# Six whole-array tiles instead of four in the prologue of a dense squared-ReLU kernel, taken row tile by row tile, with w1's first chunks on ScalarE's queue

## Chip, cores, metric

One core of a Trainium2 chip. Kernels are compared only within the same rounds. The metric is the device time of one execution in microseconds (us). An execution's time is about 1.75 us longer than the span that the profile shows (290.45 against 288.7 for the profiled run of the kernel before).

## The reference

```python
B, S, D, F = 1, 2048, 576, 4608          # all bf16
def reference(x, w1, b1, w2, b2):
    h = jnp.einsum("bsd,df->bsf", x, w1) + b1
    r = jnp.where(h > 0, h, 0)
    h = r * r
    return jnp.einsum("bsf,fd->bsd", h, w2) + b2
```

## The kernel before

F is cut into 36 tiles of 128 columns ("f-tiles"), S into four blocks of 512 rows. The first phase makes h for all f-tiles of each block, the second multiplies by w2. D = 576 is 4.5 times 128, so the usual form of the first product is row-split: two f-tiles run side by side on the two 64-row halves of the array, nine chunks of 64 each (`a_step`, which comes down to line L213 in the profile). That form needs x transposed and in two halves. For block 0 x has to be transposed on the spot, so its first G = 4 f-tiles take a whole-array form: four chunks of 128 rows and one paired 64-row rest. They need less data and let the row-split weights arrive meanwhile.

```python
    load_x(nc.sync, 0)
    load_x(nc.scalar, 1)
    load_quad(nc.sync, 0)          # w1 rows of chunk c, columns of the first G f-tiles
    load_quad(nc.scalar, 1)
    load_quad(nc.sync, 2)
    load_x(nc.scalar, 2)
    load_x(nc.sync, 3)
    load_quad(nc.scalar, 3)
    nc.scalar.activation(out=warm[:], in_=..., func=ACT.Relu)     # brings the table load forward
    # ... (cut: the 64-row rest, then the row-split w1 chunks on SyncE, pair by pair)
    for i in range(NWARM):         # NWARM = 5: matmuls of ones while x is on its way
        nc.tensor.matmul(wps[:], lhsT=ones[:, 0:P], rhs=ones[:], start=(i == 0), stop=(i == NWARM - 1))

    def transpose_chunks(half, cs, engs):      # half = two row tiles of x
        tps = [psum.tile([P, HALF], BF16, name="tp", tag="bank") for c in cs]
        for i in range(2):
            for c, tp in zip(cs, tps):
                d0 = c * P if c < NC else D - P
                nc.tensor.transpose(tp[:, i * P:(i + 1) * P], xs[:, 2 * half + i, d0:d0 + P], ident[:])
        # ... (cut: copies from PSUM into xT[0])
    def full_mm(half, c):                      # 256 columns, G f-tiles
        for q in range(4):
            nc.tensor.matmul(bk0[q][:, cols], lhsT=qn[:, c, q * P:(q + 1) * P], rhs=xT[0][:, c, cols], ...)

    transpose_chunks(0, (0,), (V,))
    transpose_chunks(0, (1,), (A,))
    transpose_chunks(0, (2,), (A,))
    transpose_chunks(0, (NC,), (V,))
    full_mm(0, 0)
    transpose_chunks(0, (3,), (A,))
    full_mm(0, 1)
    # ... (cut: the rest in the same manner, b1's transpose, the paired 64-row rest, evictions)
    for j in range(2, NJ):
        a_step(0, j)
```

All PSUM tiles (PSUM is the memory that TensorE writes to) come from one pool of eight banks; a bank is free again when VectorE or ScalarE has copied its contents out.

## Time and profile before

| | |
|---|---|
| median of the first three runs | 290.14 us (289.88 to 290.80) |
| span of the profiled run | 288.7 us |
| TensorE busy | 284.9 us (99%) |
| first transpose, first row-split matmul | 2.71 us, 9.62 us |
| array goes from half to full clock | 5.95 us (the trace's clock record) |

In the timeline a line is: start, length, engine, source line, operation, operands, count, and in brackets idle time with what ended it. For TensorE the length includes draining, so two starts are subtracted to get a pitch: two 512-column matmuls of ones start 0.43 us apart at half clock, and row-split pairs 0.216 us apart at full clock. "tp" are transposes, "ph" accumulating matmuls, "wps" the warm-up; PE is TensorE, DVE VectorE, ACT ScalarE, and SP SyncE. The row "PEclk" of the page does not show the half clock of the start; its record begins at the switch. The pitch of the matmuls shows it.

### The profile page before, as it was taken

Reading aid. Unit: us, or ns where it says so; the run is one execution under the profiler, and the core shown is the slowest. Engines: PE = TensorE matmul, PEld = TensorE weight load, DVE = VectorE, ACT = ScalarE, POOL = GpSimd, SP = SyncE. Lnnn points to the kernel's source line nnn. Section 1 sums busy time; section 2 is a strip of 40 time slices with the busy share of each in tenths; the row PEclk is TensorE's granted clock in tenths of the full one; section 3 lists DMA queues with packets and bytes.
Section 4 is the critical chain, followed back from the end, with each engine's and each line's share of the span. In section 5 each row is a group of like instructions: output and inputs, shape, how many; then the busy total and the mean of one; then the engine's idle time right before and its main releaser. Section 6 shows DMA issues by size and latency. Waiting matters only on the chain.

```text
span 288.7 us, 4818 instructions
## 1 busy us (share of the span) xinstructions
PE 284.9 (99%) x2067; PEld 133.7 (46%) x2078; DVE 79.5 (28%) x196; ACT 95.6 (33%) x153; POOL 1.5 (1%) x8
## 2 busy tenths in 40 slices
PE   9999999999999999999999999999999999999996
PEld 5544444444444444444445444444444444444454
DVE  1644454444445444444420011111100111111111
ACT  3666666766666676666620000000000000000000
POOL 2000000000000000000000000000000000000000
PEclk9999999999999999999999999999999999999999
DMA  7999999910400004300000100000000000000000
GB/s 200 205 190 204 172 185 208 321 50 2 122 3 0 3 2 142 106 0 2 0 2 19 20 20 20 20 23 5 15 20 23 20 20 20 23 20 22 20 23 20
DMA packets 35381, 18.01 MB, mean 62 GB/s; under 512 B 21652, under 2 KB 35360, under 8 KB 35360
## 3 DMA queue, kind: packets, MB, share of 16 engines
q1 hardware_dynamic: 34752, 17.14, 26.4%
q10 hardware_dynamic: 576, 0.56, 0.6%
q8 instruction: 16, 0.26, 0.4%
q14 instruction: 5, 0.04, 0.0%
q0 software_dynamic: 32, 0.01, 0.0%
HBM read 11.94 MB, written 2.36 MB: 50 GB/s over the span
## 4 chain that ended last, share of the span: by engine, by line
PE 98%; DMA 1%; issue 0%; DVE 0%; ACTq 0%
PE ph L213 47%; PE po L329 43%; PE pc L315 5%; PE ph L228 2%; DMA w_sb<-in_x_dram 1%; PE tp L182 1%; PE ph L254 0%; DVE o_sb L331 0%; PE b1T_ps L247 0%; ACTq L353 0%
## 5 line engine op out<-in xcount | busy, mean ns | idle before, releaser
L197 ACT ACTIVATE r<-ph,b1T 128x512 bf16<-128x512 f32 x144 | 91.0, 685 | 48.4 <-PE ph L213 46.4
L213 PE MATMUL ph<-w_sb,w1h 64*128 64x512 bf16 x936 | 101.2, 376 | 0.0
L213 PEld LDWEIGHTS <-w1h 64*128 64x128 bf16 x1260 | 61.3, 94 | 74.6
L329 PE MATMUL po<-w_sb,hT 128*128 128x512 bf16 x423 | 92.9, 379 | 0.5
L329 PEld LDWEIGHTS <-hT 128*128 128x128 bf16 x432 | 42.2, 98 | 51.2 <-issue 0.4
L199 DVE TENSOR_TENSOR hT<-r 128x512 bf16<-128x512 bf16 x108 | 46.0, 426 | 54.7 <-ACT r L197 54.2
L331 DVE TENSOR_TENSOR o_sb<-po,b_bc 128x512 bf16<-128x512 f32 (+2 forms) x17 | 11.2, 660 | 116.7 <-PE po L329 109.7
L213 PE MATMUL ph<-xT,w1h 64*128 64x512 bf16 x324 | 35.1, 376 | 0.0
L329 PE MATMUL po<-w_sb,w1h 128*128 128x512 bf16 (+2 forms) x178 | 31.2, 336 | 0.1
L329 PEld LDWEIGHTS <-w1h 128*128 128x128 bf16 x180 | 16.2, 98 | 15.3
L199 DVE TENSOR_TENSOR w1h<-r 128x512 bf16<-128x512 bf16 x36 | 15.3, 426 | 19.6 <-ACT r L197 19.5
L315 PE MATMUL pc<-hT,w_sb 128*64 128x512 bf16 x108 | 15.7, 379 | 0.0
L315 PEld LDWEIGHTS <-w_sb 128*64 128x64 bf16 x144 | 8.1, 110 | 7.6 <-issue 0.4
L315 PE MATMUL pc<-w1h,w_sb 128*64 128x512 bf16 x36 | 7.9, 379 | 0.0
L317 ACT ACTIVATE oc<-pc,b2T 128x512 bf16<-128x512 f32 x2 | 1.4, 687 | 13.7 <-PE pc L315 13.7
L325 DVE COPY o_sb<-oc 128x64 bf16<-128x64 bf16 x16 | 2.8, 172 | 9.3 <-DMA oc<-oc 9.3
L228 PE MATMUL ph<-w_sb 128*128 128x256 bf16 x32 | 5.3, 313 | 0.0
L228 PEld LDWEIGHTS <-w_sb 128*128 128x128 bf16 x32 | 3.4, 115 | 0.6
L175 DVE COPY w_sb<-tp 128x256 bf16<-128x256 bf16 x5 | 1.5, 292 | 5.9 <-PE tp L182 5.9
L182 PE MATMUL tp<-ident,w_sb 128*128 128x128 bf16 x20 | 2.7, 264 | 0.1
L169 PE MATMUL wps<-one 128*128 128x512 bf16 x5 | 2.3, 628 | 0.4 <-DVE one L144 0.4
L182 PEld LDWEIGHTS <-w_sb 128*128 128x128 bf16 x20 | 1.9, 118 | 1.4 <-DMA w_sb<-in_x_dram 1.2
(27 smaller groups left out, 10.7 us busy)
## 6 DMA issues: line engine op xcount, KB each, us to landing
w_sb<-in_w_dram SPq DMA_DIRECT2D x2, 1728.0 KB, 8.7
w1h<-in_w_dram SPq DMA_DIRECT2D x8, 288.0 KB, 5.9
out_dram<-o_sb SPq DMA_DIRECT2D x15, 144.0 KB, 1.8
w1h<-in_w_dram SPq DMA_DIRECT2D x12, 144.0 KB, 3.7
w_sb<-in_w_dram SPq DMA_DIRECT2D x2, 864.0 KB, 7.2
w1h<-in_w_dram SPq DMA_DIRECT2D x2, 576.0 KB, 11.2
w_sb<-in_x_dram SPq DMA_DIRECT2D x2, 144.0 KB, 3.4
w_sb<-in_x_dram ACTq DMA_DIRECT2D x2, 144.0 KB, 3.5
```

What stands on the lines that cost most here:

```text
L169: nc.tensor.matmul(wps[:], lhsT=ones[:, 0:P], rhs=ones[:], start=(i == 0), stop=(i == NWARM - 1))
L175: nc.vector.tensor_copy(out=dst, in_=src)
L182: nc.tensor.transpose(tp[:, i * P:(i + 1) * P], xs[:, 2 * half + i, d0:d0 + P], ident[:])
L197: nc.scalar.activation(out=r[:], in_=bk[:], func=ACT.Relu, bias=b1T[:, ft:ft + 1], scale=1.0)
L199: nc.vector.tensor_tensor(out=hT_of(b, ft), in0=r3, in1=r3, op=ALU.mult)
L213: nc.tensor.matmul(bk[h][:], lhsT=w1h[rows, c, j * P:(j + 1) * P], rhs=xT[b][rows, place(h, c), :], start=(i == 0), stop=(i == NH - 1))
L228: nc.tensor.matmul(bk0[q][:, cols], lhsT=qn[:, c, q * P:(q + 1) * P], rhs=xT[0][:, c, cols], start=(half == 0 and c == 0), stop=False, ski ...
L315: nc.tensor.matmul(pc[h * H:(h + 1) * H, :], lhsT=w2(ft, DM, D), rhs=hT_of(2 * pr + h, ft), start=(ft == 0), stop=(ft == NFT - 1))
L317: nc.scalar.activation(out=oc[:, pr, :], in_=pc[:], func=ACT.Identity, bias=b2T[:], scale=1.0)
L325: nc.vector.tensor_copy(out=o_sb[:, DM:D], in_=o_tr[pr][:, jj, h * H:(h + 1) * H])
L329: nc.tensor.matmul(po[:, 0:e - a], lhsT=hT_of(b, ft)[:, jj, :], rhs=w2(ft, a, e), start=(ft == 0), stop=(ft == NFT - 1))
L331: nc.vector.tensor_tensor(out=o_sb[:, a:e], in0=po[:, 0:e - a], in1=b2_bc[:, a:e], op=ALU.add)
```

## The change

Its intent: run six f-tiles in the whole-array form, so that the row-split weights are wanted later; begin as soon as row tile 0 of x is there; put other matmuls between a tile's transposes and their first use; and ask for w1's chunks from ScalarE while SyncE asks for x.

```diff
-    G = 4
+    G = 6
+    GP = G // 2
-    load_x(nc.sync, 0)
-    load_x(nc.scalar, 1)
-    load_quad(nc.sync, 0)
-    load_quad(nc.scalar, 1)
-    load_quad(nc.sync, 2)
-    load_x(nc.scalar, 2)
-    load_x(nc.sync, 3)
-    load_quad(nc.scalar, 3)
+    for j in range(RT):
+        load_x(nc.sync, j)
+        load_quad(nc.scalar, j)
 ... (pairs and the row-split chunk list follow: single chunks for j = 3 to 9)
+    def transpose_tile(j, c, n, eng):          # row tile j, n chunks into one bank
+        ...
+    transpose_tile(0, 0, 1, V)
+    transpose_tile(0, 3, 1, V)
+    transpose_tile(0, 1, 2, A)
+    transpose_tile(0, NC, 1, V)
     bk0 = [bank("ph") for _ in range(G)]
+    full_mm(0, 1, 0)                           # row tile, number of row tiles, chunk
+    transpose_tile(1, 0, 2, V)
+    transpose_tile(1, 2, 2, A)
+    full_mm(0, 1, 1)
+    full_mm(1, 1, 0)
+    full_mm(1, 1, 1)
+    transpose_tile(2, 0, 2, V)
+    transpose_tile(2, 2, 2, A)
+    full_mm(0, 2, 2)
+    full_mm(2, 1, 0)
+    transpose_tile(1, NC, 1, V)
+    full_mm(2, 1, 1)
+    transpose_tile(3, 0, 2, V)
+    transpose_tile(3, 2, 2, A)
+    full_mm(2, 1, 2)
+    full_mm(0, 2, 3)
 ... (cut: the rest of row tile 3, b1, the paired 64-row rest)
-    for j in range(2, NJ):
+    for j in range(GP, NJ):
         a_step(0, j)
```

## The prediction

> **What bounds the kernel now.** I read the page first: busy time, the slices, then the chain that ended last.
>
> ```profile
> span 288.7 us, 4818 instructions
> PE 284.9 (99%) x2067; PEld 133.7 (46%) x2078; DVE 79.5 (28%) x196; ACT 95.6 (33%) x153; POOL 1.5 (1%) x8
> PE   9999999999999999999999999999999999999996
> PE 98%; DMA 1%; issue 0%; DVE 0%; ACTq 0%
> ...
> L213 PE MATMUL ph<-w_sb,w1h 64*128 64x512 bf16 x936 | 101.2, 376 | 0.0
> ```
>
> The reader is to see that TensorE is never free after the start: the chain is 98% TensorE, and the row-split matmuls of the first phase (L213) wait 0.0 us in all. Nothing that the change touches lies after the first of 18 steps of block 0, so only the first microseconds can move. For those I asked for the chain in time order, 0 to 30 us, and for TensorE's timeline of the same stretch.
>
> ```profile
> 0.21 2.84 DMA w_sb<-in_x_dram
> 3.04 0.05 issue
> 3.09 0.93 PE tp L182 x7
> 4.02 0.85 PE ph L228 x4
> 4.87 0.21 PE tp L182 x2
> 5.09 1.36 PE ph L228 x8
> 6.45 0.22 PE tp L182 x4
> 6.67 0.44 PE ph L228 x4
> ...
> 9.24 0.54 PE ph L254 x4
> 9.78 20.29 PE ph L213 x187
> ```
>
> The first rows are the arrival of x; from 3.09 us on every row is TensorE. The four 256-column matmuls at 4.02 us take 0.85 us (0.21 each), the four at 6.67 us take 0.44 (0.11 each). So the array runs at half speed until about 6 us; the trace's clock record puts the switch at 5.95 us. Evictions and weight arrivals do not show as waits:
>
> ```profile
> 2.71 1.31 PE L182 MATMUL tp<-ident,w_sb 128*128 128x128 bf16 x8
> 3.81 1.06 PE L228 MATMUL ph<-w_sb 128*128 128x256 bf16 x4
> 4.67 0.42 PE L182 MATMUL tp<-ident,w_sb 128*128 128x128 bf16 x2
> 4.88 1.57 PE L228 MATMUL ph<-w_sb 128*128 128x256 bf16 x8
> ...
> 9.17 0.60 PE L254 MATMUL ph<-w_sb 64*128 64x512 bf16 x4
> ```
>
> From start to start, there are three holes on TensorE: the last warm-up matmul starts at 2.06 and streams 0.43 us, so 2.49 to 2.71 is empty (0.22 us, row tile 0 of x lands); 2.82 to 3.09 (0.27 us; the second transpose wants row tile 1, which lands at 3.04); and about 0.09 us before 9.17. That is all an ideal reordering could win: 0.58 us of 290, or 0.2%. Two of the holes lie at half clock, where a hole costs half its length in full-speed work (if the switch stays at 5.95).
>
> **What the Trainium skill says.** "TensorE: Matmul & The Clock Gate", Part 1 (The HAM clock gate): the array is at half clock until a window of about 3.4 us has been busy; the window runs freely and "doesn't reset when your kernel starts", so the switch moves from run to run. The trace agrees on the two speeds (0.21 and 0.11 us) and has the switch at 5.95 us; that it moves, one trace cannot show, but the three times spread over 0.9 us. "DMA: Bandwidth & Descriptors", Issuing engines are not separate DMA queues: transfers started by ScalarE and SyncE run on the same 16 DMA engines and interleave. The trace agrees: both queues' packets alternate from 1.8 us on, and together move 331 GB/s from 1.8 to 4.2 us. The same page, Why small descriptors are slow, says that short descriptors pay a fixed overhead: here the first loads, with 1,024 and 1,152 B pieces, make those 331 GB/s, the later w1 chunks with 256 B pieces 196 GB/s (9.6 to 21.6 us).
>
> **The change part by part.**
>
> Work on TensorE. Before, one whole-array f-tile costs 8 matmuls of 256 columns (0.1085 us start to start) and half of a paired 512-column matmul (0.216/2), 0.98 us; a row-split pair of f-tiles costs 9 x 0.216 = 1.94 us, 0.97 each. So moving two f-tiles from one form to the other is free by itself. After, block 0's six tiles need 60 matmuls of 128 columns (transposes of that width run at 0.0545 us start to start, each with its own weights, so 60 x 0.0545 = 3.27), 18 of 256 columns (1.95) and three pairs (0.65): 5.87 us. Before, the same six tiles cost 4 x 0.976 + 1.94 = 5.85. Sum: +0.02 us. The 20 transposes and the one of b1 stay.
>
> Start. Only row tile 0 of x is needed for the first five transposes, so the 0.27 us hole for row tile 1 goes. In its place the first matmuls wait for the first eviction and w1's first chunk. Five transposes at half clock: 2.71 to 3.24. The first copy starts when the first transpose has drained (2.71 + 0.29 + 0.03 = 3.03). A VectorE copy of 256 columns from PSUM takes 292 ns (L175), the 36-column cast 195; between them 128 columns make an estimate of 0.24 us, so chunk 0 is ready at 3.27 and seen by TensorE around 3.33. w1's first chunk is now first on ScalarE's queue, where row tile 1 landed at 3.04 before; it has 197 KB for 147, an estimate of 3.2. The hole is 3.24 to about 3.4, 0.16 us instead of 0.27. Gain, at half clock: 0.06 us.
>
> Middle. The six accumulating banks leave two of eight for transposes, and the built program makes each new transpose wait for the eviction two before it. I walked the order with 0.107 us (cold) and 0.0545/0.1085 us (warm) per matmul. Tile 1's transposes at about 4.04 meet ScalarE's first copy, which cannot start before its warm-up ends at 3.63 and takes 0.37: ready at 4.05, a hole of at most 0.05. Tile 3's second pair of transposes meets a real one: the remainder transpose of tile 1 starts at about 7.4, drains by 7.6, and its two copies on VectorE (2 x 0.24) free the bank at 8.1, while TensorE has only 6 matmuls and 2 transposes in between (0.33 + 0.11) and stands there at 7.88. Hole: 0.2 us at full clock. The others (b1's transpose, tile 2's remainder) come out within 0.1 us of even.
>
> DMA. The first loads grow from 1,114 KB to 1,376 KB (w1 chunks of 768 columns instead of 512). At 331 GB/s that is +0.8 us, so w1's last chunk lands at about 6.6 instead of 5.9; it is first used at about 8.6, while before it was used 0.55 us after it landed. The order in which chunks are used leaves every one about a microsecond. The row-split chunks then start at pair 3, wanted at about 11.7 instead of 9.4; the bytes before the last, four-pair chunk are the same in sum, but 295 KB of them now move at 331 instead of 196 GB/s: about 0.6 us earlier. This is worth something only where a chunk is nearly late: before, the last half chunk landed at 32.69 and was read at 32.93, without a stall in this trace.
>
> Sum: +0.02 (work) - 0.06 (start) + 0.03 (tile 1) + 0.2 (tile 3) = +0.2 us, at most +0.3. The first row-split matmul should start at about 11.7, against 11.56 at which the same six f-tiles are done before. 290.14 + 0.2 would be 290.3; I take 290.2, as the DMA slack may save a stall in runs that the trace does not show.
>
> **The rivals.**
>
> First, the change hides real latency and gains its whole 0.6 us: for it speaks that x and w1 are now asked for in the order of use and that other work lies before each first use; against it, that the before trace shows no wait for an eviction on TensorE after 3.1 us. It would give 289.6.
>
> Second, the clock switch comes a window later, as narrower matmuls and holes between 2.5 and 6 us leave TensorE less busy when it is judged. For it speaks only that this stretch has more eviction waits; against it that its holes sum to 0.4 us by my walk, no more than before (0.5). A later switch by 3.4 us would cost 1.7 us: 291.9. I give it 5%.
>
> Third, DMA: heavier early loads delay row tiles 1 to 3 or push the row-split stream behind, and TensorE waits; per microsecond of delay not covered one microsecond is lost. For it speaks that SyncE's ninth load waits on the semaphore of ScalarE's first, now larger load (it waited 1.1 us before); against it the extra 2 us before the first row-split chunk is wanted. It would give 290.5 to 291.5.
>
> Fourth, a late w1 chunk already costs time in unprofiled runs before, and the 0.6 us earlier stream saves it: 289.4 to 289.8. The trace can neither show nor exclude it.
>
> **Range and chances.** A change of 2% is 5.8 us; block 0's whole prologue, up to the first row-split matmul, is 9.6 us of which 3.9 is useful work at full speed. The first rival's gain is a tenth of the 2% line and the worst rival's loss a third of it. So within 2% has 0.99, and 0.005 remains for each side. The range is set by the run-to-run spread (289.88 to 290.8 for the kernel before), widened to the low side by the first and fourth rival and to the high side by the third: 289.4 to 291.0 us around 290.2.
>
> **What would show it right or wrong.** In the changed trace: TensorE's first transposes at about 2.7; the first 128-column matmul at about 3.4, not later than 3.6; the clock switch near 6 us (a switch near 9.4 is the second rival); a wait of the second transposes of tile 3 on VectorE of about 0.2 us; L208 starting within 0.3 us of 11.7, and no idle time on it. If L208 starts before 11.3, my walk of the bank waits is too dark; if after 12.1, a DMA or a bank wait was missed. A gain over 1 us with these starts as predicted would mean that the row-split stream stalls in runs without a profile. The prediction as a whole is wrong if the median leaves the range.

## The result, and the profile after

The changed kernel took 290.31 us (median of 4 runs, 289.99 to 290.72) against 290.11 (4 runs, 289.88 to 290.80). Ratios here are the mean time of one kernel's fast runs over the mean of the other's in the same rounds, not quite the ratio of medians: 1.0004, 95% interval 0.9982 to 1.0025. Run again with five rounds it was 290.44 against 290.32, ratio 1.0002 (0.9988 to 1.0016).

The page of the changed kernel:

```profile
span 288.2 us, 4882 instructions
PE 284.2 (99%) x2097; PEld 134.3 (47%) x2108; DVE 80.4 (28%) x202; ACT 94.8 (33%) x152; POOL 1.5 (1%) x8
PE 97%; ACT 1%; issue 0%; DVE 0%
...
L208 PE MATMUL ph<-w_sb,w1h 64*128 64x512 bf16 x918 | 99.2, 376 | 0.0
```

TensorE is again 99% busy and the row-split matmuls (now L208, two f-tiles fewer in block 0) again wait 0.0 us. But ScalarE and VectorE have come into the chain that ended last. The chain in time order (start, length, what), 0 to 30 us, says where:

```profile
2.16 1.28 ACT L112
...
...
3.66 0.27 ACT w_sb L169
...
3.97 0.38 PE tp L178 x4
...
6.67 0.07 PE tp L178
...
6.76 0.23 DVE w_sb L171
...
7.00 0.24 DVE w_sb L171
...
7.28 0.29 PE tp L178 x2
...
11.22 18.78 PE ph L208 x174
```

Two holes stand here that the kernel before has not. Before 3.97 us TensorE waits for a bank that ScalarE empties, and ScalarE came late: its table load begins at 2.16 us. (It began at 2.15 in the kernel before too, but there no TensorE wait came of it.) Before 7.28 us it waits for a bank that VectorE empties with two copies in a row (6.76 and 7.00 us). The wait for row tile 1 of x, the first row of the chain before, is gone.

TensorE's timeline of the same run has two surprises:

```profile
3.30 0.49 PE L228 MATMUL ph<-w_sb 128*128 128x128 bf16 x6
3.97 0.38 PE L178 MATMUL tp<-ident,w_sb 128*128 128x128 bf16 x4 [0.18 <-ACT w_sb L169]
...
11.06 1.24 PE L208 MATMUL ph<-w_sb,w1h 64*128 64x512 bf16 x10
```

The six matmuls at 3.30 us end within 0.49 us: they run at full clock. The clock record has the switch at 3.31 us instead of 5.95. And the row-split matmuls start at 11.06, not at about 11.7. By the prediction's own test ("before 11.3") my walk of the bank waits would be too dark. It was not: the profiled run had an early switch. The same kernel profiled again gave:

```profile
2.54 0.71 PE L178 MATMUL tp<-ident,w_sb 128*128 128x128 bf16 x5
3.15 0.80 PE L228 MATMUL ph<-w_sb 128*128 128x128 bf16 x6
3.97 0.59 PE L178 MATMUL tp<-ident,w_sb 128*128 128x128 bf16 x4
...
9.41 0.50 PE L228 MATMUL ph<-w_sb 128*128 128x128 bf16 x6
9.74 0.22 PE L178 MATMUL tp<-ident,w_sb 128*128 128x128 bf16 x1
...
11.68 0.60 PE L208 MATMUL ph<-w_sb,w1h 64*128 64x512 bf16 x4
```

Same first transposes of row tile 1 (3.97), but half clock until 5.47 us and the row-split start at 11.68. So two single traces of two kernels cannot be compared without looking at this switch, and I read it from every trace.

### The profile page after: what moved, and what is told of

Read it like the earlier page. It is cut to its first block, busy times and chain, and to the rows that moved or that the text cites. A ratio compares the mean times of both kernels' runs of the same rounds, so it can differ in the third digit from the quotient of the medians.

```text
span 288.2 us, 4882 instructions
## 1 busy us (share of the span) xinstructions
PE 284.2 (99%) x2097; PEld 134.3 (47%) x2108; DVE 80.4 (28%) x202; ACT 94.8 (33%) x152; POOL 1.5 (1%) x8
## 4 chain that ended last, share of the span: by engine, by line
PE 97%; ACT 1%; issue 0%; DVE 0%
PE ph L208 47%; PE po L335 43%; PE pc L321 5%; PE ph L228 2%; ACT L112 0%; PE tp L178 0%; PE ph L259 0%; DVE w_sb L171 0%; DVE o_sb L337 0%; ACT w_sb L169 0%; ACT warm L112 0%; PE b1T_ps L253 0%
## 5 line engine op out<-in xcount | busy, mean ns | idle before, releaser
L208 PE MATMUL ph<-w_sb,w1h 64*128 64x512 bf16 x918 | 99.2, 376 | 0.0
L208 PEld LDWEIGHTS <-w1h 64*128 64x128 bf16 x1242 | 60.4, 94 | 73.6
L337 DVE TENSOR_TENSOR o_sb<-po,b_bc 128x512 bf16<-128x512 f32 (+2 forms) x17 | 11.2, 660 | 116.7 <-PE po L335 109.7
L208 PE MATMUL ph<-xT,w1h 64*128 64x512 bf16 x324 | 35.1, 376 | 0.0
L228 PE MATMUL ph<-w_sb 128*128 128x128 bf16 (+1 forms) x78 | 6.4, 231 | 0.0
L171 DVE COPY w_sb<-tp 128x128 bf16<-128x128 bf16 (+2 forms) x13 | 3.0, 239 | 6.6 <-PE tp L178 6.4
L169 ACT COPY w_sb<-tp 128x256 bf16<-128x256 bf16 x4 | 1.5, 367 | 2.9 <-PE tp L178 2.9
```

The costliest lines, as they stand in the source:

```text
L169: nc.scalar.copy(out=dst, in_=src)
L171: nc.vector.tensor_copy(out=dst, in_=src)
L208: nc.tensor.matmul(bk[h][:], lhsT=w1h[rows, c, j * P:(j + 1) * P], rhs=xT[b][rows, place(h, c), :], start=(i == 0), stop=(i == NH - 1))
L337: nc.vector.tensor_tensor(out=o_sb[:, a:e], in0=po[:, 0:e - a], in1=b2_bc[:, a:e], op=ALU.add)
```

## The experiments

Theory 1: TensorE's work is nearly the same in both kernels; the time varies with the clock switch, which falls at a different place in each run; at equal switch the changed kernel loses a few tenths of a microsecond in its two new holes. Rivals: the new order itself moves the switch; or loads decide. "Six tiles done" below is the start of the first row-split matmul, for the kernels with four whole-array tiles plus 1.94 us (9 pairs at 0.216), so that both stand for the same work. All times in us.

| run | ratio to before (95%) | switch | first transpose | six tiles done | span of the profiled run |
|---|---|---|---|---|---|
| before, first trace | | 5.95 | 2.71 | 11.56 | 288.7 |
| b_again | 0.9992 (0.9980 to 1.0004) | 5.43 | 2.65 | 11.26 | 288.4 |
| changed, first trace | 1.0004 (0.9982 to 1.0025) | 3.31 | 2.69 | 11.06 | 288.2 |
| a_again | 1.0002 (0.9988 to 1.0016) | 5.47 | 2.54 | 11.68 | 288.8 |
| a_freeact | 1.0016 (0.9992 to 1.0040) | 9.10 | 3.40 | 13.76 | 290.9 |
| a_move | 1.0000 (0.9986 to 1.0014) | 5.79 | 2.81 | 11.57 | 288.7 |
| a_both | 0.9995 (0.9983 to 1.0007) | 5.30 | 2.54 | 11.22 | 288.3 |
| a_best | 0.9998 (0.9986 to 1.0009) | 5.69 | 2.68 | 11.37 | 288.5 |
| b_nowarm | 1.0026 (1.0009 to 1.0043) | 7.77 | 2.75 | 12.46 | 289.6 |
| a_nowarm | 1.0043 (1.0029 to 1.0057) | 7.31 | 2.62 | 12.57 | 289.7 |
| b_queue | 1.0036 (1.0016 to 1.0055) | 7.49 | 2.78 | 12.53 | 289.7 |
| b_queue2 | 1.0017 (0.9995 to 1.0039) | 4.81 | 2.56 | 11.11 | 288.2 |
| b_qfill | 1.0014 (0.9995 to 1.0033) | 6.17 | 2.72 | 11.87 | 289.0 |
| a_oldqueue | 1.0062 (1.0033 to 1.0092) | 7.72 | 2.65 | 13.11 | 290.2 |

All twelve runs from b_again to a_oldqueue gave correct results.

One thing the table holds without saying it: in each of the 14 traces the span less "six tiles done" is 277.12 to 277.14 us. So whatever sets the profiled runs apart happens before that point; nothing after it, a late weight of the row-split form included, made a difference between them.

**Both kernels again, unchanged (b_again, a_again).**

> The kernel before, unchanged: noise and clock phase. Theory 1 (the half-clock switch falls anywhere, 3.3 us and 5.95 us so far, and every microsecond of it later costs about 0.5 us of time): ratio 1.000 within 0.003, and if its switch is near 3.3 us the first row-split matmul starts at about 9.0 us instead of 9.62, with a wait for row tile 3 of x and w1's last chunk (landed 5.7 to 5.9) appearing on TensorE. Rival (the switch is fixed by the kernel's own order of work): switch at 5.95 us again.

> The changed kernel, unchanged: ratio to before 1.000 within 0.003. Theory 1: the switch is elsewhere than 3.31 us; if it is near 6 us the first row-split matmul starts at about 11.7 us, not 11.06, and the two holes (0.34 us before the transposes of row tile 1, 0.27 us before the second pair of row tile 3) shrink or stay. Rival (the new order brings the switch forward): switch near 3.3 us again and 11.06 us again.

The kernel before, run again (b_again, window 2 to 12 us):

```profile
2.65 1.30 PE L182 MATMUL tp<-ident,w_sb 128*128 128x128 bf16 x8
...
9.32 2.97 PE L213 MATMUL ph<-w_sb,w1h 64*128 64x512 bf16 x26
```

The switches came at 5.43 and 5.47 us, by luck nearly equal, and so give the cleanest comparison: six tiles done at 11.26 before (9.32 plus 1.94) and 11.68 after. At equal clock the changed kernel is 0.42 us later; subtracting 0.02 for the switch leaves 0.40. (Row tile 0 came 0.11 us earlier in a_again, worth about 0.05 at half clock in its favour.) For the changed kernel the switch moved by 2.16 us between its two traces, so the order of work alone does not fix it: the rival falls in that form. Whether the order changes how often the switch comes early is not tested. In 11 runs of the kernel before made beside these, times went from 289.82 to 290.84, a spread of 1.0 us, 2.5 times the difference that the traces show.

**No warm-up (b_nowarm, a_nowarm).** To move the switch on purpose:

```diff
-    NWARM = 5
+    NWARM = 1
```

> The kernel before with one warm-up matmul in place of five (results stay right). Theory 1 (a free-running window of about 3.4 us has to be busy for some 75% before the clock doubles; seen so far: windows with 62% and 71% of TensorE's streaming time did not switch it, 80% and 87% did): TensorE is idle from 0.8 to 2.7 us, so the switch falls between about 5.4 and 8.9 us, 2 us later on average, and the time rises by about half of that: ratio 1.002 to 1.006 (0.6 to 1.7 us). Rival (the switch comes a fixed time after the first matmul, or the phase has little weight): ratio under 1.001.

> The changed kernel with one warm-up matmul in place of five. Theory 1: as for the kernel before, switch between 5.4 and 8.9 us, ratio to before 1.003 to 1.007. Holes at half clock are worth less, so its distance to the kernel before without warm-up is 0 to 0.4 us at the same phase. Rival (a row-tile-wise order needs less of a busy window): the loss is less than half of that of the kernel before without warm-up.

As expected: 290.97 and 291.48 us (medians) against 290.24, switches at 7.77 and 7.31. The timeline of b_nowarm:

```profile
2.75 1.32 PE L182 MATMUL tp<-ident,w_sb 128*128 128x128 bf16 x8 [1.76 <-DMA w_sb<-in_x_dram]
...
7.07 0.95 PE L228 MATMUL ph<-w_sb 128*128 128x256 bf16 x4
...
8.07 0.60 PE L228 MATMUL ph<-w_sb 128*128 128x256 bf16 x4
```

TensorE now stands idle before the first transpose (1.76 us), starts no later than before, and yet four 256-column matmuls still take 0.95 us at 7.07, and 0.60 a microsecond later. Between b_again and b_nowarm the switch is 2.34 us later and the six tiles 1.20: a microsecond of late switch costs 0.51 us. For the changed kernel it is 0.89 over 1.84, or 0.48. (Between its own two traces it is only 0.62 over 2.16: with the switch at 3.31 TensorE reached the ScalarE hole early and stood there until 3.97 all the same.) Brought to one switch with that slope, the changed kernel is 0.34 us behind without warm-up, inside the expected 0 to 0.4.

**Closing the two holes (a_freeact, a_move, a_both).** First, ScalarE issues two loads instead of four:

```diff
-    for j in range(RT):
-        load_x(nc.sync, j)
-        load_quad(nc.scalar, j)
+    for j in range(2):
+        load_x(nc.sync, j)
+        load_quad(nc.scalar, j)
+    for j in range(2, RT):
+        load_x(nc.sync, j)
+        load_quad(nc.sync, j)
```

> Changed kernel with w1's chunks 2 and 3 issued by SyncE, so that ScalarE has two issues instead of four. Theory 1 with its two holes: ScalarE's table load starts at about 1.2 us instead of 2.16, its first copy at about 3.3, and the hole before the transposes of row tile 1 falls from 0.34 to under 0.1 us; time lower by 0.1 to 0.3 us, too little to be clear (ratio to before 0.998 to 1.001). Rival (ScalarE is held by the start barrier and not by its issues): table load stays at 2.1 to 2.2 us and the hole stays. Second rival (chunks 2 and 3 come later and TensorE waits for them): a wait on a w1 load of 0.2 us or more appears.

Second, the rest of row tile 1 is transposed six matmuls earlier:

```diff
-    full_mm(2, 1, 0)
     transpose_tile(1, NC, 1, V)
+    full_mm(2, 1, 0)
```

> The changed kernel with the remainder transpose of row tile 1 one group of six matmuls earlier, and nothing else. Bank theory: the hole before the second pair of transposes of row tile 3 (0.27 us in both traces of the changed kernel) goes; the one before row tile 1 stays (0.34 or 0.23 us by phase). First row-split matmul about 0.27 us earlier than the changed kernel at the same switch: 11.4 us for a switch at 5.5. Time 0.2 to 0.3 us lower, within noise. Rival (a later transpose inherits the wait): a hole of the same size appears at a later transpose and the row-split start does not move.

Third, both:

> The same, and the remainder transpose of row tile 1 moved one group of six matmuls earlier, so that its two VectorE copies have 0.66 us of cover instead of 0.33. Bank theory: the hole of 0.27 us before the second pair of transposes of row tile 3 goes to 0; with the first hole gone too, the time is 0.4 to 0.6 us under the changed kernel at the same clock phase: ratio to before about 0.998 to 0.999, the fastest of the four if the phases fall alike. Rival (holes close, but the time follows the clock phase alone): holes gone in the trace and no difference in the ratio beyond 0.1%.

ScalarE's timeline in the changed kernel, then in a_both:

```profile
2.16 1.28 ACT L112 ACT_TABLE_LOAD   x1 [2.16 <-ACTq L359]
...
3.57 0.35 ACT L169 COPY w_sb<-tp 128x256 bf16<-128x256 bf16 x1
```

```profile
1.18 1.28 ACT L115 ACT_TABLE_LOAD   x1 [1.18 <-ACTq L362]
...
3.18 0.37 ACT L172 COPY w_sb<-tp 128x256 bf16<-128x256 bf16 x1 [0.50 <-PE tp L181]
```

With two issues fewer the table load begins a microsecond earlier, and the first copy now waits for TensorE (0.50 us) instead of the reverse. TensorE's timeline of a_both:

```profile
3.14 0.80 PE L231 MATMUL ph<-w_sb 128*128 128x128 bf16 x6
3.73 0.63 PE L181 MATMUL tp<-ident,w_sb 128*128 128x128 bf16 x4
...
7.34 0.39 PE L181 MATMUL tp<-ident,w_sb 128*128 128x128 bf16 x4
...
11.22 1.03 PE L211 MATMUL ph<-w_sb,w1h 64*128 64x512 bf16 x8
```

The transposes of row tile 1 follow the six matmuls at once (3.73, where a_again had 3.97 after an equal start), those of row tile 3 run in one go (0.39 instead of 0.67 us). Six tiles are done at 11.22 with a switch at 5.30. a_again began with its first transpose at the same 2.54 us and would be done at about 11.59 with that switch, so closing the two holes won 0.37 of the 0.40 us. Against b_again at 5.43 it would be about 11.29 for 11.26, or 0.08 behind with row tile 0 landing alike, the size of the extra work found below (0.09). a_move alone: the second hole is gone and does not come back elsewhere; brought to a_again's switch it stands 0.27 us earlier, the size of the hole. Its row tile 0 landed 0.26 us later, which the first hole took up: the expected wait before the transposes of row tile 1 (0.23 to 0.34) was not there (3.41 plus six matmuls, then 4.00).

In time none of this is clear of noise: 0.9995 for a_both, 1.0000 for a_move, and 1.0016 for a_freeact, outside the 0.998 to 1.001 expected of it. a_freeact closed the ScalarE hole too (its row tile 1 transposes follow without a wait), but its profiled run drew something else: row tile 0 of x arrived late. Of its 16 completion events the last came at 3.35 us, against 2.65 in the first trace of the changed kernel, TensorE began at 3.40, the switch came at 9.10 and the run took 292.64. The three loads behind it landed 0.7 to 0.8 us later as well. As a_both has the same order of loads and began at 2.54, I take this as a chance event; why the first loads were late stays open.

**All known holes closed (a_best).** a_both, with b1's transpose moved ahead by three groups:

```diff
     full_mm(0, 2, 3)
+    b1T_ps = psum.tile([P, P], BF16, name="b1T_ps", tag="bank")
+    nc.tensor.transpose(b1T_ps[:], b1_rows[:], ident[:])
+    nc.vector.tensor_copy(out=b1T[:], in_=b1T_ps[:, 0:NFT])
     ... (and removed from its later place)
```

> The changed kernel with both holes closed (w1's chunks 2 and 3 issued by SyncE, tile 1's remainder transpose earlier) and b1's transpose moved ahead by three groups, out of the wait for its bank. Theory: no hole over 0.05 us beyond the arrival of x and the change of array form; row-split start at 11.1 to 11.2 us for a switch at 5.4 (changed kernel 11.68), 0.1 us under the kernel before's equivalent 11.26; ratio to before 0.998 to 1.000, not clear of noise. Rival (a hole reappears elsewhere): row-split start at 11.4 or later for that switch.

Six tiles done at 11.37 with a switch at 5.69; at 5.43 about 11.24, just short of the expected 11.1 to 11.2: as good as the kernel before and no better. 290.25 us against 290.13. No version beats the kernel before clear of noise.

**The queue part alone, on the order before (b_queue, b_queue2, b_qfill).** Row tiles of x on SyncE, w1's chunks on ScalarE, everything else as before:

```diff
-    load_x(nc.sync, 0)
-    load_x(nc.scalar, 1)
-    ... (six more)
+    for j in range(RT):
+        load_x(nc.sync, j)
+        load_quad(nc.scalar, j)
```

> The kernel before with the queue part of the change alone: row tiles of x on SyncE, w1's chunks (still 512 columns) on ScalarE. Theory: row tile 1 is then SyncE's second load, lands at about 3.4 to 3.6 instead of 3.04, and as the second transpose of this kernel needs it, the hole on TensorE there grows from 0.27 to 0.6 to 0.8 us: the row-split start 0.2 to 0.4 us later than 9.3 (for a switch near 5.4), or a window later (up to 1.7 us more) if the bigger hole makes the window too idle. Rival (queue assignment does not matter, all land as before): hole within 0.1 us of 0.27.

> The kernel before with the queue part alone, once more, as the partner of the next run. Ratio 1.002 to 1.005 as in the first run; hole at the second transpose 0.6 to 0.8 us.

The chain of b_queue:

```profile
0.53 2.96 DMA w_sb<-in_x_dram
3.49 0.05 issue
3.54 0.93 PE tp L177 x7
```

Row tile 1, now SyncE's second load, is issued at 0.53 us, and the second transpose waits for it until 3.54, a hole of 0.65 us instead of 0.27. Times: 291.35 against 290.24 (1.0036, clear of 1), and 290.25 against 290.13 (1.0017, not clear, and under the 1.002 to 1.005 expected). The runs fall in two groups: 290.35 and below (five of ten), and 291.27 to 291.94 (the other five, one of them b_queue's profiled run with a switch at 7.49).

> The same with two idle-fill matmuls (512 and 128 columns of ones into the warm-up bank, never read) between the first and the second transpose, where TensorE stands waiting for row tile 1. They bring row tile 1 no earlier. Window theory (a window under some 75% busy does not double the clock, and the hole of 0.6 to 0.7 us costs mainly by that): the switch comes on average over a microsecond earlier than without the fill, the time falls to within 0.1% of the kernel before (ratio 0.999 to 1.002). Rival (the hole costs as lost time only): no change from the partner run, ratio 1.003 to 1.004; the wait for row tile 1 and the row-split start stay for the same switch.

```diff
                 nc.tensor.transpose(tp[:, i * P:(i + 1) * P], ...)
+                if half == 0 and i == 0 and c == 0:
+                    for n in (SB, P):
+                        nc.tensor.matmul(wps[:, 0:n], lhsT=ones[:, 0:P], rhs=ones[:, 0:n], start=True, stop=True)
```

This expectation was not shown: the ratio, 1.0014, lies in the expected range, but so does the partner's, 1.0017. One of its six runs was long (292.04), of the partner's six two. That is too few to say that the filled hole helps or does not; the trace has the fill in place (the idle part shrinks to about 0.15 us) and an ordinary switch at 6.17.

**The new order with the queues before (a_oldqueue).** The eight old load lines in the changed kernel:

> The changed kernel with the queue assignment of the kernel before: x0, w1 chunk 0, chunk 2, x3 on SyncE, x1, chunk 1, x2, chunk 3 on ScalarE. Theory: w1's chunk 0 is then third in the stream, lands at about 3.4 to 3.5 instead of 3.16, and the first 128-column matmuls, which need it, start 0.2 to 0.3 us later (3.5 to 3.6); the ScalarE hole behind them shrinks by the same amount, so the row-split start moves by 0.1 us or less at the same switch, and the time stays: ratio 0.999 to 1.002. Rival (the queue part carries the kernel, as it broke the one before): ratio over 1.002 and a wait of over 0.5 us on a w1 or x load.

A miss, and the most useful one. 292.36 us against 290.13, ratio 1.0062, the slowest kernel. Its timeline:

```profile
4.02 0.82 PE L233 MATMUL ph<-w_sb 128*128 128x128 bf16 x6 [0.65 <-DMA w_sb<-in_w_dram]
```

w1's first chunk, third in the stream, landed at 3.97 us and not at 3.4 to 3.5; the hole before the first matmuls, from 3.17 to 4.02, is 0.85 us instead of 0.1 in the changed kernel. So the two parts of the change need each other: the queues alone cost 1.0036 and 1.0017 (the second not clear of 1), the six tiles in their new order with the old queues 1.0062, both together nothing measurable.

**Why a hole of 0.7 us can cost 1.7 us.** "TensorE: Matmul & The Clock Gate" of the Trainium skill, Part 1 (The HAM clock gate), gives a free-running window of 3,413 ns. The traces agree with the length: the stretch at full clock is 283.306 us long in 13 of them and 286.720 in one, 83 and 84 times 3,413 ns. From every trace comes the share of that window, ending at the switch, in which TensorE was streaming (each matmul counted for its columns at the clock of the moment, 0.107 us for 128 at half clock), and the same for the window before it, which had not switched the clock:

```
                        window that ended at the switch   window before it
before, first trace                 87%                        62%
changed, first trace                77%                         0%
b_again / a_again               87% / 88%                  48% / 49%
a_freeact                          100%                        70%
a_move / a_both / a_best     88% / 94% / 92%            58% / 44% / 55%
b_nowarm / a_nowarm            100% / 97%                  38% / 42%
b_queue / b_queue2             100% / 79%                  72% / 30%
b_qfill / a_oldqueue            96% / 100%                 63% / 70%
```

In 14 traces no window above 72% failed to switch and none under 77% did. A hole early on pushes some windows below the line, and which ones depends on where the window happens to lie; the switch then waits a whole window, which at 0.51 us per us is an estimated 1.7 us. The three late switches with warm-up (7.49, 7.72, 9.10) all follow a window of 70 to 72%. That the slow group of runs without a trace has this same cause is an inference; so is the line itself, which was found from these traces and then fitted the later ones. (The expectation of b_nowarm has an earlier count of the same shares: 71 and 80% where the table has 70 and 77.)

## Why the prediction was right, and where its steps were off

The time, 290.31, lay in the range and 0.1 us from the point. That it lay so near is luck: at equal switch the traces give +0.40 us and not +0.2, the point itself was set 0.1 under the sum for a saving that no trace shows, and runs of one kernel spread over 1.0 us. What was right is the frame: only the first microseconds can move (everything after took 277.12 to 277.14 us in all traces), the holes there are too small to win much, and new bank waits take the gain back. By its steps:

- Work: "+0.02" was mis-sized. I used 0.0545 us as the pitch of 128-column matmuls; both kernels' traces have 0.0556 to 0.0558 (in a_again six, from 9.41 to 9.74). 60 of them make 3.34 us for 3.27, and with 0.109 for 256 columns the sum is 5.96 against 5.87: +0.09.
- Start: right in kind. The hole for row tile 1 went; the first 128-column matmul came at 3.15 to 3.30 instead of 3.4, as w1's first chunk landed at 3.16 or earlier; the hole before it was 0.1 and not 0.16.
- Middle, tile 1: "at most 0.05" was too small. The term measured 0.23 us (a_again: six matmuls end at 3.74, transposes at 3.97) and 0.34 where the clock was already full. I had ScalarE's time nearly right (4.05 for 3.97), but TensorE came earlier than I thought, and what it gains ahead of ScalarE's start-up is lost in that wait.
- Middle, tile 3: "0.2" measured 0.27 in all traces of the changed kernel. b1's bank: within 0.1, measured 0.08.
- Sum: +0.2, against +0.40 at equal switch. A check from the measured terms of a_again: +0.09 work, +0.11 (0.23 at half clock), +0.27, +0.08, less 0.13 (0.27 at half clock), less 0.05 for an earlier x: +0.37.
- DMA: not shown. w1's last chunk landed at 6.23 us in the first trace of the changed kernel and at 7.05 in a_again (6.6 predicted). The last row-split half chunk landed at 30.97 against 32.69 in the first traces, but at 30.74 against 30.23 in a_again and b_again, so "0.6 us earlier" is smaller than the scatter of one kernel. No TensorE wait depended on it after the prologue in any trace, so the fourth rival gets no support.
- DMA rates: the larger first loads moved at 375 GB/s and not 331 (1.8 to 4.2 us). And the later, slower stream was misread: in the trace before, pieces of 256 B moved at 205 and 209 GB/s (9.6 to 12, 12 to 14 us) and pieces of 512 B at 200 (18 to 21.6 us), so the size of the pieces is not shown to be what holds it at 196.
- Second rival: given 5% and not seen in the two traces of the changed kernel, but it is what the slow traces of both half-changes show (switches at 7.49 and 7.72). I had named the right mechanism and put the wrong weight on how near the kernel stands to it.
- Range: taken from the run-to-run spread, whose cause I quoted (the free-running window) without using it. At half a microsecond per microsecond, a switch anywhere in one window of 3.4 us makes a spread of 1.7 us; the 11 runs beside b_again covered 1.0.

## What to carry to other kernels

When TensorE is 99% busy, an added overlap has nothing to hide, and a reordering can only exchange holes; count the holes of the kernel before first, since at an equal clock switch their sum is the most that can be won. Read the clock switch (the pitch of the first matmuls) in every trace before two of them are compared: here it moved one kernel by 0.6 us, more than the whole change. Load order and order of use are one decision: each half of this change alone cost 0.2 to 0.6% (the 0.2 not clear of noise), together they cost nothing measurable.

## What the Trainium skill lacked or had wrong

- "TensorE: Matmul & The Clock Gate", Part 4 (PE-mode transpose) says that transposes do not count as busy for the clock "the same way". Here they count: the first trace of the changed kernel switched after a window with 62% of matmuls, nearly all of them warm-up, and 15% of transposes, while the window before the switch of the first trace of the kernel before had the same 62% and no transposes, and did not switch. Leaving transposes out, switching windows go down to 55% and failing ones up to 62%.
- The same page, Part 1, does not say how busy a window has to be. The 14 traces put the line between 72% (no switch) and 77% (switch).
- The same page, Back-to-back issue gap, gives about 81 ns per matmul for a sustained stream of weight loads and 128-column matmuls, and 131 ns for 512 columns. These runs show 55.6 to 55.8 ns for 128 columns with new weights each time, and 216 ns for the whole-array 512-column matmuls of the second phase, also with new weights. What the section calls the isolated gap, about 56 and 216 ns, is what this stream of weight loads and matmuls keeps.
- "DMA: Bandwidth & Descriptors", Issuing engines are not separate DMA queues, calls the sequencer's time to start a transfer usually small relative to the transfer. It is here too (0.38 to 0.46 us for an issue against 2.9 to 4.6 to the landing, ScalarE's four in the first trace of the changed kernel), but the section does not say that the issuing engine's own work waits behind its issues: four of them put ScalarE's table load at 2.16 us, two at 1.18, and the four made TensorE wait 0.23 to 0.34 us.
